# An earlier end of one block's attention and another dealing of the last logits, in a fused attention, gated product and expert kernel

## The chip, the cores and the metric

The kernel runs on one core of one Trainium2 chip. Its time is the device time of one execution in microseconds (us), and the median of several executions is compared. Before the change it is 1007.12 us (three runs, 1005.93 to 1008.37). The profile of before is of an execution of its own that took 1008.56 us.

## The reference

Three layers follow each other, on 3072 tokens (4 batches of 768) of width 512 (8 heads of 64):

```python
for t in range(S):                                   # decayed linear attention
    state = gamma * state + einsum('bhd,bhe->bhde', k[:, :, t], v[:, :, t])
    y[:, :, t] = scale * einsum('bhd,bhde->bhe', q[:, :, t], state)
x = y in (token, head*dim) order                     # 3072 x 512
x = ((x @ w_a) * (x @ w_b)) @ w_out                  # d_ff 1536
e_idx = argmax(x @ w_gate)                           # top 1 of 8 experts
gate_w = softmax(x @ w_gate)[e_idx]
eom = sigmoid(x @ w_output_gate)[e_idx]
out[token] = gate_w * eom * (relu(x @ w1[e_idx]) @ w2[e_idx])   # d_ff 1024
```

All in fp32 accuracy. The choice of the expert depends on small differences of logits, so the kernel works at that accuracy all the way to them.

## The kernel before

**Products.** Every fp32 operand of a big product is split into a high part that TensorE takes in one pass and a low part (the rest). `mm3` then makes three matmuls of each (lines 111, 112 and 113: high by high, high by low, low by high). A split is a cast on ACT and a subtraction on DVE: for the x of a block `split` in `x_steps` (ACT L695, DVE L696), for the gated product `gate` (DVE L579 and L587, ACT L584), for an expert's weights L462 and L463.

**Blocks.** The tokens are four blocks: two of 512 tokens and two of 1024. A loop over j handles the first two blocks. For each of the 12 slices f of d_ff it makes the *up products*: `proj` by w_a (12 matmuls), then by w_b (12), the gate, and `down` of the f before (12 matmuls into four accumulators). After each of these three stands a `slot()`: 36 slots in a loop. At a slot, `spread` hands out steps of other work. Each line of steps has a first and a last slot, and at slot s a step is handed out while the share of steps done is less than the share of the way between the two. The steps of a line are closures that issue instructions, so this decides the place of each instruction in every engine's program. Nothing is moved afterwards: each engine works through its own list in order.

**What is handed out in the loop j=1.** The attention of block 2 (`attention_steps(2)`: scores sc, mask m, state, outputs y on PE, copies on ACT, joins `xraw<-xraw,y` and the decayed operands qd and vd on DVE or POOL) and the routing of the first 512 tokens, `route(0, 4, False)`: 32 dot products for the logits on DVE (`dot`, L342), then `s_m` (largest logit, choice, index ix, exp, counters), then a gather from `w_output_gate` by ix for each tile of 128 tokens (`s_g`, an indirect DMA on POOL, tile wx), a dot product with what it brought (`s_o`, L342 again), and the rest (`s_e`; `s_r`, a rank matmul rp at L401; `s_s`, the scatter into a table tab_d).

**Blocks of sums.** The two blocks of 1024 tokens use a product of sums: seven products of quarters in place of eight, with x operands B11, B21, U1, U2, B22, U3 and U4. `x_steps` forms U1 to U4 by subtractions on DVE (L690) and splits all seven. `block_of_sums` makes, for each f, the seven products (6 matmuls each) with the `down` tiles of f-1 between them, and a slot after each: 84 slots. The sums a, b and later on DVE (L748, L770, L776, L787) release the two accumulators p0 and p1 to the next products. Each product of block 2 also needs a `unit`, sums of the weights (POOL makes wsum, ACT L664 and DVE L665 split it). `later_pass` does the other half of the down product. In before, x of block 2 is formed at slots 27 to 31 (B21 and B11), at the end of the last f (five steps) and in the first slots of the block of sums (four steps).

**Last logits.** The logits of the last 512 tokens are made on PE (`route(20, 4, True)`: transposes pt, products lp, ACT copies lg, then `s_m` and so on), one step after each half of the up products of expert 0's first 256 rows (`up2`), whose tokens are known by then. Then two turns (PE transposes pg of a gathered tile xg, L887, the split ACT L889 and DVE L890) of the next rows of expert 0, which need the table's index (idx, DMA from tab_d) and the gather xg from x. `load_expert` splits the expert's weights (L462, L463) and loads the ones after next.

## Time and profile before

| | |
|---|---|
| median of three runs | 1007.12 us |
| profiled execution, its own time | 1008.56 us |
| span of its profile | 1006.5 us |
| mean granted TensorE clock over the span | 0.987 of full speed |
| PE busy | 962.7 us (96%) |
| DVE busy | 602.6 us (60%) |
| ACT busy | 361.9 us (36%) |
| POOL busy | 249.9 us (25%) |
| DMA moved | 217.58 MB |

Read it so: PE is busy for all but some 44 us of the span, and a part of the rest is at the start and the end. So what is to be looked at are the single waits of PE in the middle, each named with the engine that ended it, and the stretches in which the granted clock fell after them. In the rows below, a number in brackets is the idle time of the engine before an instruction, with what ended it; PEclk is the granted clock as a share of full speed (2.4 GHz; 0.5 is the lower level, 1.2 GHz).

### The profile page before, as it was taken

The page shows a single profiled execution, that of the slowest core. Times are in us where ns is not written, and L with a number is a line of the kernel's source. Part 1 is how long each engine was busy: PE and PEld are TensorE (multiplying, and loading weights), DVE is VectorE, ACT ScalarE, POOL GpSimd, SP SyncE. Part 2 cuts the span into 40 slices and gives each one's busy share as a digit, 9 for nine tenths or more (in the row PEclk, how much of TensorE's full clock was granted, in tenths as well). Part 3 has the DMA queues.
Part 4 walks back from the last instruction along what each step waited for, and adds up shares of the span by engine and source line. Part 5 has one row for each costly group of instructions (what it writes and reads, how often), then busy time and mean ns, then how long its engine had stood idle before and what let it go on. Part 6 is the DMA issues. An engine that isn't in the chain of part 4 may idle for free. (4 is left out here: it accounts for less than half of the span.)

```text
span 1006.5 us, 19402 instructions
## 1 busy us (share of the span) xinstructions
PE 962.7 (96%) x7248; PEld 797.6 (79%) x7249; DVE 602.6 (60%) x1213; ACT 361.9 (36%) x668; POOL 249.9 (25%) x238
## 2 busy tenths in 40 slices
PE   6899999998889999999999999999899999999997
PEld 5688888886678777878787787878799988889886
DVE  4899966785655777657386586444365544445531
ACT  2677752222322222334211112333354434344431
POOL 4211002124434554520012212221321120221311
PEclk9899999999999999999999999999899999999999
DMA  6999979786379876828666865471564552545620
GB/s 237 352 326 310 312 261 359 242 271 243 143 257 374 282 236 227 258 107 295 226 234 210 282 237 180 166 212 45 179 213 136 175 177 86 186 143 155 212 73 29
DMA packets 77253, 217.58 MB, mean 216 GB/s; under 512 B 13230, under 2 KB 22702, under 8 KB 75569
## 3 DMA queue, kind: packets, MB, share of 16 engines
q1 hardware_dynamic: 69840, 196.34, 57.7%
q0 software_dynamic: 6704, 18.93, 5.5%
q8 instruction: 82, 1.34, 0.5%
q10 hardware_dynamic: 576, 0.56, 0.2%
q14 instruction: 51, 0.41, 0.1%
HBM read 165.41 MB, written 51.30 MB: 215 GB/s over the span
## 5 line engine op out<-in xcount | busy, mean ns | idle before, releaser
L941 DVE TENSOR_TENSOR ew<-wraw,ew 128x512 fp32r<-128x512 f32 x112 | 77.1, 690 | 56.0 <-ACT ew L940 55.5
L342 DVE SCALAR_TENSOR_TENSOR junkd<-x2r,wcol 128x512 bf16<-128x512 f32 x128 | 99.9, 780 | 2.4
L111 PE MATMUL acc<-xe,ew 128*128 128x384 f32 (+4 forms) x288 | 98.4, 342 | 0.6 <-issue 0.6
L905 DVE SCALAR_TENSOR_TENSOR hs<-acc,hs 128x384 fp32r<-128x384 f32 (+4 forms) x72 | 39.0, 542 | 98.4 <-ACT hs L904 98.4
L113 PE MATMUL acc<-xe,ew 128*128 128x384 f32 (+4 forms) x288 | 95.4, 331 | 0.0
L112 PE MATMUL acc<-xe,ew 128*128 128x384 f32 (+4 forms) x288 | 95.3, 331 | 0.0
L111 PE MATMUL p<-U,unit 128*128 128x512 f32 x192 | 78.1, 407 | 11.8 <-ACT a L742 4.2
L940 ACT CAST ew<-wraw 128x512 fp32r<-128x512 f32 x112 | 68.8, 616 | 56.9 <-PE acc L113 52.8
L927 POOL DMA_INDIRECT out<-y,idx x27 | 27.4, 1016 | 230.2 <-ACT y L926 154.5
L777 POOL TENSOR_TENSOR later<-later,b 128x512 f32<-128x512 f32 x24 | 37.5, 1563 | 173.8 <-DVE b L776 173.8
L111 PE MATMUL p<-xs,ar 128*128 128x512 f32 x192 | 78.2, 408 | 0.1
L113 PE MATMUL p<-xs,ar 128*128 128x512 f32 x192 | 76.1, 396 | 0.0
L112 PE MATMUL p<-xs,ar 128*128 128x512 f32 x192 | 75.9, 395 | 0.0
L111 PE MATMUL acc<-wos,gs 128*128 128x512 f32 x192 | 75.8, 395 | 0.0
L113 PE MATMUL p<-U,unit 128*128 128x512 f32 x192 | 75.5, 393 | 0.0
L112 PE MATMUL p<-U,unit 128*128 128x512 f32 x192 | 75.4, 393 | 0.0
L904 ACT ACTIVATE hs<-acc 128x384 fp32r<-128x384 f32 (+4 forms) x72 | 34.4, 478 | 113.9 <-PE acc L113 113.7
L113 PE MATMUL acc<-wos,gs 128*128 128x512 f32 x192 | 74.9, 390 | 0.0
L112 PE MATMUL acc<-wos,gs 128*128 128x512 f32 x192 | 74.8, 390 | 0.0
L789 ACT CAST gs<-a 128x512 fp32r<-128x512 f32 x24 | 14.9, 621 | 138.2 <-DVE a L787 127.0
L111 PE MATMUL p<-B,unit 128*128 128x512 f32 x144 | 57.5, 399 | 2.0 <-DVE a L787 2.0
L111 PEld LDWEIGHTS acc<-xe,ew 128*128 128x128 f32 x288 | 54.6, 189 | 3.8 <-issue 1.0
(201 smaller groups left out, 2277.8 us busy)
## 6 DMA issues: line engine op xcount, KB each, us to landing
wraw<-in_ex SPq DMA_DIRECT2D x64, 512.0 KB, 4.1
wos<-wos_d SPq DMA_DIRECT2D x39, 512.0 KB, 5.9
wide<-in_w_ab SPq DMA_DIRECT2D x24, 512.0 KB, 5.5
q_d<-unit SPq DMA_DIRECT2D x24, 512.0 KB, 6.4
unit<-q_d SPq DMA_DIRECT2D x12, 1024.0 KB, 5.7
qk<-in_qk SPq DMA_DIRECT2D x23, 512.0 KB, 6.3
vk<-in_vk SPq DMA_DIRECT2D x23, 512.0 KB, 7.0
q_d<-ar SPq DMA_DIRECT2D x36, 256.0 KB, 4.8
```

Of the source, the lines that this page charges most:

```text
L111: pe.matmul(outp, lhsT=wh, rhs=rh, start=start, stop=False, skip_group_check=more)
L112: pe.matmul(outp, lhsT=wh, rhs=rl, start=False, stop=False, skip_group_check=more)
L113: pe.matmul(outp, lhsT=wl, rhs=rh, start=False, stop=stop, skip_group_check=more)
L342: dve.scalar_tensor_tensor(junk, x, 1.0, y, op0=ALU.mult, op1=ALU.mult, accum_out=out)
L777: pool.tensor_tensor(g2, g2, b2, op=ALU.mult)
L789: act.copy(gs[:, 0], a1)
L904: act.activation(h[:, 0, :n], p[:, :n], AF.Relu)
L905: dve.scalar_tensor_tensor(h[:, 1, :n], p[:, :n], 0.0, f32(h[:, 0, :n]), op0=ALU.max, op1=ALU.subtract)
L927: st = pool.indirect_dma_start(out=out[:, :], out_offset=bass.IndirectOffsetOnAxis(ap=ix[:, 1:2], axis=0), in_=y, in_offset=None, bounds_c ...
L940: act.copy(ew[f][:, part, 0], t[:, part])
L941: dve.tensor_tensor(ew[f][:, part, 1], t[:, part], f32(ew[f][:, part, 0]), op=ALU.subtract)
```

## The change

1. In the loop j=1 the attention's last slot is 25 in place of 30. `x_first` (B21, B11) has slots 22 to 25, and `x_rest` (the nine other steps of x) is a line of its own with slots 26 to 34. No step of x is left at the end of the last f or in the block of sums.
2. The second half of `s_m` becomes a step of its own, `s_c`. Where the logits come from DVE, the gathers of wx are followed by more empty steps before the dot products that read them: five between the first pair's dots and the second pair's.
3. In `block_of_sums` the last f makes down tile 2 of f-1 between U3 and U4, and only tile 3 after U4.
4. In block 2 the attention of block 3 and the routing have slots 0 to 78 and 12 to 82.
5. In the last logits one step is handed out after each quarter of the up products for f = 0 and 1, after every second quarter from f = 2. The loads of the weights of slices 5 to 7 are steps among them, and the two turns come after all up and down products, one right behind the other.

```diff
--- before.py
+++ after.py
@@ -352,6 +352,13 @@
             dve.tensor_reduce(top, first, op=ALU.max, axis=AX.X)
             oh = st["oh"] = small("oh", BF16)
             dve.tensor_tensor(oh, first, over_e(top), op=ALU.is_equal)
+            st["mx"] = mx
+            if not by_pe:
+                ix = st["ix"] = small("ix", I32, (4,))
+                dve.tensor_scalar(ix, top, -1.0, 8.0, op0=ALU.mult, op1=ALU.add)
+
+        def s_c():
+            l8, mx, oh = lg[:, :, :8], st.pop("mx"), st["oh"]
             less = small("less")
             dve.tensor_tensor(less, l8, over_e(mx), op=ALU.subtract)
             ex = st["ex"] = small("ex")
@@ -361,9 +368,6 @@
                 dve.tensor_tensor(both, lg[:, :, 8:], oh, op=ALU.mult)
                 st["og"] = small("og", shape=(4,))
                 dve.tensor_reduce(st["og"], both, op=ALU.add, axis=AX.X)
-            else:
-                ix = st["ix"] = small("ix", I32, (4,))
-                dve.tensor_scalar(ix, top, -1.0, 8.0, op0=ALU.mult, op1=ALU.add)
             cs = st["cs"] = small("cs", BF16)
             dve.tensor_copy(cs[:, 0], ohsum)
             for t in range(1, n):
@@ -433,18 +437,18 @@
             out = [bank((s_t, 0))]
             for t in range(1, n):
                 out.append(bank((s_t, t), (s_l, t - 1)))
-            return out + [bank((s_l, n - 1)), s_m, s_e, bank((s_r,)), s_s]
+            return out + [bank((s_l, n - 1)), s_m, s_c, s_e, bank((s_r,)), s_s]
         out = [lambda: (s_w(), s_x()), s_w] + [none] * 6
         for e in range(E):
             for t in range(n):
                 out.append(lambda t=t, e=e: dot(st["x2", t], cols[e // 2][:, e % 2], lg[:, t, e : e + 1]))
             if e % 2:
                 out.append(s_w)
-        out += [lambda: (s_m(), s_g(0), s_g(1)), none, none, none]
+        out += [lambda: (s_m(), s_g(0), s_g(1)), none, s_c] + [none] * 4
         for t in range(n):
             out.append(lambda t=t: (s_o(t), t + 2 < n and s_g(t + 2)))
-            if t % 2:
-                out += [none, none]
+            if t == 1:
+                out += [none] * 5
         return out + [s_e, bank((s_r,), (s_s,))]
 
     rawq = {}
@@ -779,8 +783,8 @@
                 low1()
                 load_weights(f + 2)
             slot()
-            if f and not last:
-                down(j, f - 1, [2, 3])
+            if f:
+                down(j, f - 1, [2] if last else [2, 3])
             if last:
                 gd = later_split(KEPT[0])
             product(q, u, 0, "U4", False)
@@ -790,7 +794,7 @@
             dve.tensor_tensor(gs[:, 1], a1, f32(gs[:, 0]), op=ALU.subtract)
             gt[j, f] = gs
             if last:
-                down(j, f - 1, [2, 3])
+                down(j, f - 1, [3])
             if fresh:
                 store_unit(2 * f + 2)
             else:
@@ -1147,10 +1151,10 @@
 
         for j in range(2):
             n, tiles = 512, [3, 0, 1, 2] if j else [0, 1, 2, 3]
-            lines = [(attention_steps(j + 1), 0, 30)]
+            lines = [(attention_steps(j + 1), 0, 25 if j else 30)]
             if j:
                 x_first, x_rest = x_steps(2)
-                lines += [(route(0, 4, False), 2, 30), (x_first, 27, 31)]
+                lines += [(route(0, 4, False), 2, 31), (x_first, 22, 25), (x_rest, 26, 34)]
             slot, flush = spread(lines)
             for f in range(NF1):
                 last = f == NF1 - 1
@@ -1191,9 +1195,6 @@
                     flush()
                     if j == 0:
                         split_x(1, n)
-                    else:
-                        for s in x_rest[:3]:
-                            s()
                 if f > 0:
                     down(j, f - 1, tiles)
                 if j == 0:
@@ -1205,8 +1206,6 @@
                 if last:
                     if j:
                         make_unit(1)()
-                        for s in x_rest[3:5]:
-                            s()
                         next_wos()
                     down(j, f, tiles)
                 slot()
@@ -1218,7 +1217,7 @@
 
         sync.dma_start(wos_d[NF1 - 1], f32(wos[1, NF1 - 1]))
         store_unit(1)
-        slot, flush = spread([(x_rest[5:], 0, 4), (attention_steps(3), 4, 78), (route(4, 4, False), 14, 82)])
+        slot, flush = spread([(attention_steps(3), 0, 78), (route(4, 4, False), 12, 82)])
         gd = block_of_sums(2, slot)
         flush()
 
@@ -1257,7 +1256,7 @@
         hs = {}
         nothing = lambda: None
         todo = route(20, 4, True)
-        todo = [*todo[:6], nothing, todo[6], nothing, *todo[7:], count]
+        todo.insert(-2, nothing)
 
         def after():
             load_idx0(2)
@@ -1270,23 +1269,24 @@
         def sizes_known():
             n_e.extend(nc.values_load(cnt[0:1, e : e + 1], min_val=0, max_val=T) for e in range(E + 1))
 
-        todo += [after, *[nothing] * 6, sizes_known, lambda: turn((0, 2), xst(0), 0), lambda: turn((0, 3), xst(0), 128)]
-
         def next_todo():
             if todo:
                 todo.pop(0)()
 
+        todo += [count, nothing, lambda: load_expert(5), nothing, nothing, lambda: load_expert(6), nothing, after]
+        todo += [lambda: load_expert(7), *[nothing] * 8, sizes_known, lambda: turn((0, 2), xst(0), 0), lambda: turn((0, 3), xst(0), 128)]
+        load_expert(4)
         for f in range(NF2 + 1):
             if f < NF2:
-                up2(f, xst(0), LEAD, LEAD, ks=range(2))
-                next_todo()
-                up2(f, xst(0), LEAD, LEAD, ks=range(2, KD))
-                hs[f] = relu(f, LEAD)
-                next_todo()
+                for k in range(KD):
+                    up2(f, xst(0), LEAD, LEAD, ks=[k])
+                    if f < 2 or k % 2:
+                        if k == KD - 1:
+                            hs[f] = relu(f, LEAD)
+                        next_todo()
             if f > 0:
                 down2(f - 1, hs.pop(f - 1), [128, 128], 2)
                 next_todo()
-            load_expert(f + 4)
         while todo:
             todo.pop(0)()
         y = ytile()
```

Three places show how the instructions move; between them the order is the same but for such shifts. The first is DVE at the end of the up products, from the join of the attention's output to the splits of x (B is B21 and B11, og<-x2r,wx the dot products with the gathered rows; g_sb and gs are a gate). Before:

```order
L253 TENSOR_TENSOR xraw<-xraw,y 128x2x2x64 x2
L152 TENSOR_TENSOR qd<-qk,dec 128x512
L161 TENSOR_TENSOR vd<-vk,vtab 128x512
L579 TENSOR_TENSOR g_sb<-p_3090,a_sb 128x512
L587 TENSOR_TENSOR gs<-g_sb,gs 128x512
L342 SCALAR_TENSOR_TENSOR junkd,og<-x2r,wx 128x512 x2
L220 TENSOR_TENSOR m<-sc,mask 128x256 x2
L223 TENSOR_TENSOR state<-state,sc 128x128 x4
L342 SCALAR_TENSOR_TENSOR junkd,og<-x2r,wx 128x512 x2
L696 TENSOR_TENSOR B_3204<-xraw,B_3204 128x1024
L579 TENSOR_TENSOR g_sb<-p_3207,a_sb 128x512
```

After:

```order
L358 TENSOR_SCALAR ix<-top 128x4
L700 TENSOR_TENSOR B_3092<-xraw,B_3092 128x1024
L253 TENSOR_TENSOR xraw<-xraw,y 128x2x2x64 x2
L363 TENSOR_TENSOR less<-lg,mx 128x32
L372 COPY cs<-ohsum 128x8
L374 TENSOR_TENSOR cs<-cs,oh 128x8 x3
L375 TENSOR_TENSOR ohsum<-cs,oh 128x8
L700 TENSOR_TENSOR B_3159<-xraw,B_3159 128x1024
L583 TENSOR_TENSOR g_sb<-p_3185,a_sb 128x512
L591 TENSOR_TENSOR gs<-g_sb,gs 128x512
L342 SCALAR_TENSOR_TENSOR junkd,og<-x2r,wx 128x512 x2
L694 TENSOR_TENSOR xraw<-xraw 128x1024 x2
```

The last join L253 stood behind all four dot products (it is the row after this piece and the two of its gate); now it stands ahead of them, both splits and a gate are between the index ix and the first two of them, and U1 and U3 are formed behind these.

The second place is DVE where the up products end and the first f of the block of sums begins (U is the split of U1 to U4, L665 or L669 a unit of weights, L748 or L752 the sum a). Before:

```order
L665 TENSOR_TENSOR unit<-wsum,unit 128x2x256
L579 TENSOR_TENSOR g_sb<-p_3390,a_sb 128x512
L587 TENSOR_TENSOR gs<-g_sb,gs 128x512
L690 TENSOR_TENSOR xraw<-xraw 128x1024 x2
L696 TENSOR_TENSOR U_3412<-xraw,U_3412 128x1024
L665 TENSOR_TENSOR unit<-wsum,unit 128x2x256
L690 TENSOR_TENSOR xraw<-xraw 128x1024
L696 TENSOR_TENSOR U_3430<-xraw,U_3430 128x1024
L607 COPY x_3450<-acc_2155 128x512
L696 TENSOR_TENSOR B_3481<-xraw,B_3481 128x1024
L748 TENSOR_TENSOR a_3473<-a_3473,p_3466 128x512
```

After:

```order
L700 TENSOR_TENSOR U_3369<-xraw,U_3369 128x1024
L694 TENSOR_TENSOR xraw<-xraw 128x1024
L669 TENSOR_TENSOR unit<-wsum,unit 128x2x256
L700 TENSOR_TENSOR U_3406<-xraw,U_3406 128x1024
L583 TENSOR_TENSOR g_sb<-p_3409,a_sb 128x512
L591 TENSOR_TENSOR gs<-g_sb,gs 128x512
L669 TENSOR_TENSOR unit<-wsum,unit 128x2x256
L611 COPY x_3460<-acc_2197 128x512
L220 TENSOR_TENSOR m<-sc,mask 128x256 x2
L223 TENSOR_TENSOR state<-state,sc 128x128 x3
L752 TENSOR_TENSOR a_3483<-a_3483,p_3476 128x512
```

Between the last gate and the first sum a stood six subtractions and splits of 1024 columns, a unit and a copy, and three more of x behind it; now all of x stands before the last gate, and behind this come a unit, a copy, and m and state of block 3's attention.

The third place is ACT in the last logits (ew is a split of weights, hs the relu of an up product, cnt the sizes of the experts, xe the cast of a turned tile, y an output). Before:

```order
L462 CAST ew<-wraw 128x2x512
L904 ACTIVATE hs<-acc_7135 128x256
L462 CAST ew<-wraw 128x2x512
L904 ACTIVATE hs<-acc_7134 128x256
L904 ACTIVATE hs<-acc_7135 128x256
L904 ACTIVATE hs<-acc_7134 128x256
L1271 TENSOR_LOAD cnt x8
L889 CAST xe<-pg 128x4x128
L904 ACTIVATE hs<-acc_7135 128x256
L889 CAST xe<-pg 128x4x128
L926 ACTIVATE y<-p_7218,idx 128x512
```

After:

```order
L466 CAST ew<-wraw 128x2x512
L908 ACTIVATE hs<-acc_7134 128x256
L466 CAST ew<-wraw 128x2x512
L908 ACTIVATE hs<-acc_7135 128x256
L466 CAST ew<-wraw 128x2x512
L908 ACTIVATE hs<-acc_7134 128x256
L908 ACTIVATE hs<-acc_7135 128x256
L1270 TENSOR_LOAD cnt x8
L893 CAST xe<-pg 128x4x128 x2
L930 ACTIVATE y<-p_7255,idx 128x512
```

The two casts xe stood one relu apart, the first of them ahead of the relu of the last up product; now both stand behind the sizes and the last relu, one right behind the other.

## Rows read from the trace of the kernel before

**Rows 1.** Page, part 1: busy us, share of the span, instructions.

```profile
PE 962.7 (96%) x7248; PEld 797.6 (79%) x7249; DVE 602.6 (60%) x1213; ACT 361.9 (36%) x668; POOL 249.9 (25%) x238
```

**Rows 2.** PE timeline, 240 to 285: start, length, idle before, releaser.

```profile
241.11 0.39 PE L112 MATMUL acc<-wos,gs 128*128 128x512 f32 x1
...
241.33 0.39 PE L113 MATMUL acc<-wos,gs 128*128 128x512 f32 x1
...
245.54 0.18 PE L401 MATMUL rp<-oh,tri 128*128 128x32 bf16 x1 [3.81 <-DVE xraw L253]
...
272.86 0.50 PE L111 MATMUL p<-U,unit 128*128 128x512 f32 x1 [3.65 <-ACT a L742]
...
275.67 0.80 PE L111 MATMUL p<-U,unit 128*128 128x512 f32 x1 [0.38 <-DVE a L748]
...
284.63 0.47 PE L111 MATMUL p<-U,unit 128*128 128x512 f32 x1 [2.69 <-issue]
```

**Rows 3.** Windows: us, PE, PEld, DVE, ACT, POOL busy, PEclk, DMA, GB/s.

```profile
246.00:250.00 4.00, 4.00 (x12) 3.14 (x11) 1.90 (x6) 0.01 (x1) 2.52 (x2) 0.57 0.66 199
273.00:277.00 4.00, 3.62 (x9) 2.42 (x10) 3.21 (x4) 2.29 (x3) 0.00 (x0) 0.57 0.87 335
709.00:714.00 5.00, 4.88 (x19) 4.53 (x20) 1.81 (x3) 1.56 (x3) 0.00 (x0) 0.52 0.72 250
```

**Rows 4.** DVE timeline, 238 to 270, columns as in rows 2.

```profile
238.97 1.34 DVE L342 SCALAR_TENSOR_TENSOR junkd<-x2r,wx 128x512 bf16<-128x512 f32 x1 [4.79 <-DMA wx<-in_wog,ix]
...
241.34 0.69 DVE L342 SCALAR_TENSOR_TENSOR junkd<-x2r,wx 128x512 bf16<-128x512 f32 x1 [1.02 <-DMA wx<-in_wog,ix]
...
245.07 0.75 DVE L253 TENSOR_TENSOR xraw<-xraw,y 128x256 f32<-128x256 f32 x2
...
268.03 1.76 DVE L690 TENSOR_TENSOR xraw<-xraw 128x1024 f32<-128x1024 f32 x1
```

**Rows 5.** The tile wx: its gathers' time from issue to landing.

```profile
DMA to landing us min/median/max: 3.3/4.2/7.8
```

**Rows 6.** Line L152 on DVE: ns min/median/max, first and last start.

```profile
L152 DVE TENSOR_TENSOR qd<-qk,dec x10: 681/684/1835, 5.3 to 226.6; 128x512 f32<-128x512 f32 x10
```

**Rows 7.** Windows, one f of the up products, columns as rows 3.

```profile
213.50:224.00 10.50, 10.50 (x106) 8.30 (x104) 9.40 (x29) 1.91 (x4) 2.46 (x2) 1.00 0.72 240
```

**Rows 8.** PE timeline, both blocks of sums, their waits.

```profile
442.41 0.50 PE L111 MATMUL p<-U,unit 128*128 128x512 f32 x1 [0.85 <-DVE b L776]
...
557.30 0.50 PE L111 MATMUL p<-B,unit 128*128 128x512 f32 x1 [0.70 <-DVE a L787]
...
620.81 0.50 PE L111 MATMUL p<-B,unit 128*128 128x512 f32 x1 [1.30 <-DVE a L787]
```

**Rows 9.** PE timeline, expert 0's first rows.

```profile
702.56 0.28 PE L113 MATMUL acc<-xe,ew 128*128 128x256 f32 x1
...
709.12 1.08 PE L887 MATMUL pg<-ident,xg 128*128 128x128 f32 x4 [6.28 <-DMA xg<-x_d,idx]
...
715.69 0.28 PE L111 MATMUL acc<-xe,ew 128*128 128x256 f32 x1
```

**Rows 10.** DVE timeline, last logits and the turns.

```profile
687.59 1.22 DVE L463 TENSOR_TENSOR ew<-wraw,ew 128x1024 fp32r<-128x1024 f32 x1 [3.83 <-ACT ew L462]
...
691.94 1.21 DVE L463 TENSOR_TENSOR ew<-wraw,ew 128x1024 fp32r<-128x1024 f32 x1
...
693.83 0.17 DVE L413 CAST si<-sf 128x4 int32<-128x4 f32 x1
...
710.86 0.69 DVE L890 TENSOR_TENSOR xe<-pg,xe 128x512 fp32r<-128x512 f32 x1 [10.06 <-ACT xe L889]
```

**Rows 11.** ACT timeline, last logits and the turns.

```profile
686.44 0.17 ACT L323 COPY lg<-lp 128x16 f32<-128x16 f32 x1 [2.11 <-PE lp L322]
...
710.24 0.59 ACT L889 CAST xe<-pg 128x512 fp32r<-128x512 f32 x1 [9.90 <-PE pg L887]
```

**Rows 12.** POOL timeline, the gather of the first 128 rows.

```profile
705.60 0.99 POOL L865 DMA_INDIRECT xg<-x_d,idx  x1 [5.63 <-DMA idx<-tab_d]
```

## The prediction, made before the changed kernel ran

> **What bounds the kernel now.** The page's first part comes first: PE is busy for 96% of the span, and DVE, the next, for 60% [rows 1]. So the time is the length of PE's program plus PE's waits. The change adds and removes no matmul, and only waits, and what the clock does after them, can move. The second view is the list of PE's waits, followed in the PE timeline to their places. Four of them lie where the change works: 3.81 us ahead of the rank matmul at the end of the up products; 3.65, 0.38 and 2.69 us in the first f of the block of sums [rows 2]; 0.85, 0.70 and 1.30 us inside the blocks of sums [rows 8]; and 6.28 us ahead of the first turn in the last logits [rows 9]. The third view is the windows behind the long waits: for 4.0 us after the first, 4.0 us around the second and 5.0 us after the last the granted clock was 0.57, 0.57 and 0.52 on average, which is mostly the lower level of 1.2 GHz [rows 3]. PE was working at full clock before each of them and had stood still for 3 to 6 us. So a long wait costs twice: itself, and the lost part of the clock, 4.0 us of work x 0.43 = 1.7, 3.62 x 0.43 = 1.6 and 5.0 x 0.48 = 2.4 us.
>
> **Why these waits are there.** The first: the DVE timeline shows DVE standing 4.79 and 1.02 us for the gathered rows wx, in front of its dot products [rows 4]. Behind them in DVE's program stand a split of x, a gate and the last join of the attention, and PE's rank matmul, which takes the accumulator bank that this join's operand frees, came when it was done (245.07 + the first part of its 0.75). The gathers take 3.3 to 7.8 us from issue to landing [rows 5], and three hand-outs were between their issue and their reader. The second: DVE and ACT are forming x (subtractions and splits of 1.2 us and more each [rows 4, 10]) just when PE needs the sums that free its two accumulators. The last: the table's scatter follows si at 693.83 [rows 10], the index load and the gather of xg follow that, and the gather is issued at 705.60 after 5.63 us of waiting for the index [rows 12]; PE's up products had ended at 702.56 + 0.28 = 702.84 [rows 9].
>
> **The sum, part by part** (of the profiled execution, 1008.56 us, of which the span is 1006.5).
>
> *End of the up products.* The last join stands ahead of the dot products now, so the 3.81 us go with the 1.7 us of clock behind it: 5.5 us. What is late next: at the new density of steps (attention over 25 slots in place of 30) the scores of the next step come at three places only one product, 12 matmuls of 0.22 to 0.23 us [rows 2], 2.8 us, after the outputs of the step before. In those 2.8 us must fit a copy on ACT, a join of 0.75 [rows 4], and qd and vd of 0.68 each [rows 6]; with about 0.6 for the copy (a 512-column cast takes 0.59 [rows 11]) these are 2.7. Each place can cost from 0 (DVE free) to 1.2 us (qd at its longest, 1.835 [rows 6]); I take 0.3 each, near the median, about 1.0 in all. Net 4.5, between 1.9 and 5.5.
>
> *Start of the block of sums.* All nine steps of `x_rest` stand before the last gate. The 3.65 + 0.38 + 2.69 = 6.7 us and the 1.6 us of clock can go: 8.3 us. Late next are two things. U4 of the first f follows U3 with no down tile between (as for every first f), and must wait for the sum b: about as at the last f of a block, 0.85 [rows 8], I take 0.9. And the last gate has the split of U3, a subtraction, a unit and the split of U4 ahead of it on DVE, each about 1.2 us (a 1024-column split takes 1.21 or 1.22 [rows 10]), some 4.9 us against the 2.8 us of the product beside them; the down product of f = 10 (2.8 us more) hides most, 0.7 us may show (0 to 1.5). Net 6.7, between 5.5 and 8.0.
>
> *Blocks of sums.* The last f had 0.85 us of waiting for b [rows 8] in block 2 and the same in block 3; a down tile (3 x 0.23 = 0.7 us) now lies between: 2 x 0.7 = 1.4. The waits of 0.70 and 1.30 us for a [rows 8] come from dot products that stood for wx; with more empty steps in between both go, 2.0. Against it: attention and dots sit in other slots, and a burst of m, state and a dot before b's sum costs as much as such waits do now; 0.9. Net 2.5, between -0.5 (bursts at four places more) and 4.5.
>
> *Last logits.* Ahead of the last logits' product stand 9 fewer up matmuls of 0.12 and no down matmuls in place of 6 of 0.23: 2.4 us, of which I take 2, since each product now follows its transpose's copy closely. So the last lg, at 686.44 [rows 11], comes at 684.5. The split that stood ahead of the largest logit (from 687.59 for 1.22 us) goes too, and another (691.94, 1.21 us) that stood between it and si [rows 10]. The choice can start at 684.7 in place of 688.8, and si comes 4.1 + 1.2 = 5.3 us earlier; I take 4.6, because relu steps stay between. All that follows si hangs on DMAs and moves along: the turn that started at 709.12 [rows 9] could start at 704.5. PE has from 702.84 still 6 up matmuls (0.7) and 12 down matmuls (2.8) ahead of the turns, which now stand last: 706.3. So the wait of 6.28 and the 2.4 us of clock go: 8.7. What comes: the second turn's cast on ACT (0.59 [rows 11]) and its low part on DVE (0.69 [rows 10]) with their handing over, 1.9 us, are followed at once by up products that read them, where before 12 down matmuls lay between; and the logits' four products can each wait some 0.1 us (0 to 0.3) for their copies, 0.4. Net 6.4, between 1.2 (the gather not earlier, below) and 7.5. Checked from the end: the up products behind the turns start at 706.3 + 1.0 for two turns + 1.9 = 709.2 in place of 715.69 [rows 9], 6.5 earlier.
>
> Sum: 4.5 + 6.7 + 2.5 + 6.4 = 20.1. The profiled execution would take 1008.56 - 20.1 = 988.5. The median of before is 1.44 below its profiled execution, so the forecast is **987.0 us**.
>
> **What hides the moved DVE work.** All steps of x are DVE instructions of 1.2 us and now run in slots 22 to 34, beside attention, gates and dots. They cost nothing only while DVE keeps up. In the busiest f of the up products DVE is at work for 9.40 of 10.5 us, and PE for all of it at full clock [rows 7]. A fifth more attention per slot, if attention is as much as half of DVE's work there, makes 0.9 us: 10.3 of 10.5. So there is just room, and the cover is thin. What could break it the trace shows in single rows: the subtraction took 1.76 us at 268.03 [rows 4], against 1.2 for splits of the same size, and qd once 1.835 against a median of 0.684 [rows 6], while POOL was at work. The Trainium skill speaks against the move here: its GPSIMD Engine Reference (Key points) says that GpSimd shares its SBUF interfaces with VectorE and contends with VectorE instructions that have two SBUF inputs, as all of these have. By that rule each of the eleven steps of x could take up to 0.54 us longer beside POOL (1.76 - 1.22), 6 us of DVE's time; the rows agree in single cases. My sum takes 0 of it for PE, since no PE instruction but a gate's down product reads behind these steps, and keeps the rest for the rivals.
>
> **The rivals.** (a) *The gather is not earlier.* The index load and gather wait for something other than si (SP's loads of weights, or the landing of the scatter). Then xg comes at 709.1, PE arrives at 706.3 and waits 2.8 us, pays the 2.4 of clock and the 2.3 of new waits: the term is 8.7 - 7.5 = 1.2 in place of 6.4, and the time 992.2. For it: 8 us lie between si and the landed index already. Against it: that chain's start moves by two splits that can be seen. Chance 0.13. (b) *wx still comes late and holds the splits.* DVE stands 4.8 + 1.0 us [rows 4] at the first dots as before, now in front of U1 to U4; the last gate and the first products come late by what the 1 us of slack per f does not take back, about 5.4: 992.4. Gathers of up to 7.8 us [rows 5] speak for it, the distance against it: a slot is some 3.5 us [rows 7], and seven of 62 steps over 29 slots are 11.5 us, where four of 58 over 28 were 6.8. 0.10. (a) and (b) together: 997.6, 0.05. (c) *Slower: DVE becomes the bound in slots 4 to 34.* It decides from the point where DVE's work per f passes PE's 10.5 us. To eat the 20.1 us in the seven f's from slot 4 to 24 it must pass by 2.9 us per f, 13.4 us of DVE work; five stretched instructions per f (qd's 1.15 or the subtraction's 0.54 more) reach 10.3 + 2.7 to 10.3 + 5.8 = 13.0 to 16.1 only if all are at or over such a stretch. With 3.6 per f it is 987.0 + 25 = 1012. The median 0.684 of qd speaks against it. 0.04. (d) *It does not do what it says:* the waits move on to the next instruction at each of the four places and the clock falls there all the same: 1007, 0.03.
>
> **How the numbers follow.** Forecast 0.65, (a) 0.13, (b) 0.10, both 0.05, (c) 0.04, (d) 0.03. The likeliest case by itself reaches, with the bounds above added as independent, from 982.5 to 991.5. For 8 in 10 the range takes in (a) and (b) and part of both: 981.5 to 996. About 0.2%, 2 us, can be told from no change; all cases but (c) and (d) are further below, with some of (d) and a mixture of small sums at no change: faster 0.92, same 0.04, slower 0.04.
>
> **What would show it.** Right: no wait of PE over 1.5 us between the last three f's of the up products and the second f of the block of sums, and a granted clock of 1.0 throughout there; the join ahead of the dots; si near 689 less what the earlier parts gave; PE going from the last down product into the turns with no idle time, then one wait of nearly 2 us for xe. Wrong: the outputs of the attention waiting for joins at the new density, DVE idle for wx in front of U1, or the turn still waiting for xg. If the up products from slot 4 to 24 are longer than before with PE waiting on qd, vd or a gate, (c) is the case.

## The result and the profile after

The changed kernel took 998.64 us in the middle of three runs (994.58 to 998.73), where before took 1007.75 beside it: a ratio of 0.9895, with an interval from 0.9855 to 0.9935. Three disturbed runs in the whole record (1587.19 us here, 1587.86 and 5390.08 in two of the experiments) are left out of every time and ratio. So the changed kernel is faster by some 1%, and not by the 2% forecast; 987.0 with a range of 981.5 to 996 was said. Its profiled execution took 998.64 us, with a span of 996.5 in place of 1006.5. The page's first part answers to [rows 1]; PE's work is the same, and its share 97%:

```profile
PE 965.0 (97%) x7248; PEld 797.7 (80%) x7249; DVE 609.2 (61%) x1213; ACT 362.8 (36%) x668; POOL 249.6 (25%) x238
```

The first view to make is a table of stages. Each begins with a matmul that both traces have: the first up product, the first B21 of the block of sums, the B21 of its third f, the first product of a later pass, the first up product of expert 0, PE's last matmul. The lengths are differences of their starts in the PE timelines; the last line goes to the end of the last matmul.

| stage, us | before | changed | difference | forecast |
|---|---|---|---|---|
| both loops of up products | 238.97 | 235.21 | -3.8 | -4.5 |
| block 2, first two f | 34.51 | 26.79 | -7.7 | -6.7 |
| block 2, ten other f | 144.44 | 147.59 | +3.2 | |
| later pass of block 2 | 35.48 | 36.77 | +1.3 | |
| block 3 | 152.38 | 150.24 | -2.1 | -2.5, of these three |
| later pass of block 3 | 43.61 | 46.46 | +2.9 | 0 |
| last logits and experts | 323.89 | 320.89 | -3.0 | -6.4 |

The first two lines are what was forecast, 11.5 us for 11.2. The other five were to bring 8.9 us and cost 2.3. Where they went stands in the PE timeline of the changed kernel; these are the larger of its waits from the end of the up products on (in brackets the idle time and what ended it):

```profile
258.08 0.49 PE L111 MATMUL acc<-wos,gs 128*128 128x512 f32 x1 [0.35 <-ACT gs L588]
...
273.67 0.51 PE L111 MATMUL p<-U,unit 128*128 128x512 f32 x1 [0.78 <-DVE b L780]
...
399.96 0.50 PE L111 MATMUL p<-U,unit 128*128 128x512 f32 x1 [2.68 <-DVE a L752]
...
438.74 0.50 PE L113 MATMUL acc<-wos,gs 128*128 128x512 f32 x1 [0.44 <-DVE gs L794]
...
611.63 0.50 PE L111 MATMUL p<-B,unit 128*128 128x512 f32 x1 [1.37 <-DVE a L791]
...
658.92 0.47 PE L111 MATMUL p<-wos,gd 128*128 128x512 f32 x1 [1.89 <-DMA wos<-wos_d]
...
700.87 1.79 PE L891 MATMUL pg<-ident,xg 128*128 128x128 f32 x8 [1.91 <-issue]
...
703.34 0.58 PE L111 MATMUL acc<-xe,ew 128*128 128x256 f32 x1 [0.68 <-ACT xe L893]
```

The waits of 3.81, 3.65, 0.38 and 2.69 us of [rows 2] are gone, and so is the 6.28 of [rows 9]. New are 2.68 us for the sum a at 399.96 and 1.91 + 0.68 us at the turns; the wait at 658.92 was 1.20 us in before:

```profile
667.49 0.47 PE L111 MATMUL p<-wos,gd 128*128 128x512 f32 x1 [1.20 <-DMA wos<-wos_d]
```

The windows show which of them cost twice (us, PE, PEld, DVE, ACT and POOL busy, granted clock, DMA share, GB/s):

```profile
262.00:300.00 38.00, 37.22 (x401) 29.70 (x402) 16.04 (x32) 11.30 (x23) 15.96 (x18) 1.00 0.94 328
399.00:405.00 6.00, 5.04 (x15) 4.00 (x16) 1.20 (x4) 1.62 (x3) 0.09 (x1) 0.72 0.26 81
658.00:664.00 6.00, 5.08 (x17) 4.02 (x18) 1.64 (x2) 0.65 (x2) 2.14 (x3) 0.72 0.75 146
700.00:708.00 8.00, 6.31 (x28) 5.65 (x29) 2.47 (x4) 2.15 (x4) 3.02 (x3) 0.57 0.61 200
```

The start of the block of sums runs at full clock throughout, where [rows 3] had 0.57. But at each of these three waits the clock fell to 1.2 GHz, for 3.4, 3.4 and 6.8 us. So waits of 1.9 to 2.7 us, with their clock, are the missing gain, and the experiments ask for the cause of each.

### The profile page after: what moved, and what is told of

Its sections match the earlier page's. It is cut to its first block, busy times and chain, and to the rows that moved or that the text cites. A ratio compares the mean times of both kernels' runs of the same rounds, so it can differ in the third digit from the quotient of the medians.

```text
span 996.5 us, 19406 instructions
## 1 busy us (share of the span) xinstructions
PE 965.0 (97%) x7248; PEld 797.7 (80%) x7249; DVE 609.2 (61%) x1213; ACT 362.8 (36%) x668; POOL 249.6 (25%) x238
```

## The experiments

Kernels that ran together share their runs of before, in three sets: 1009.54 us for the changed kernel again, s_c later, the load of slice 7 and the dummy work; 1013.54 for the sizes, the old logits, the steps of x and the first run of the joined kernel; 1009.83 for the other four. Times of different runs are therefore compared by their ratio to before; a ratio compares executions that ran side by side, so it is not the quotient of the two medians. Most of these ratios differ by less than their intervals, so what decides an experiment is the length of a stage and the rows in it.

**The changed kernel again.**

> The changed kernel once more, for its spread. Theory: of the 20 us forecast some 10 are missing at three places, each a wait of PE of 1.9 to 2.7 us that also pulls the granted clock down: 2.68 us for the sum a in f = 9 of block 2 (4.2 us with the clock), 1.89 us for a weight load in the later pass of block 3 (1.7 us more than the 1.20 of before, with the clock 2.9), and 1.91 + 0.68 us at the two turns (2.4 us of clock behind them). Set by the order of the instructions, the first and the last come again within 0.5 us; the middle one hangs on a transfer and may come with 1.2 us and no fall of the clock, 994 to 996 us then, else 998 to 999. Rival (chance): the waits lie elsewhere in another execution and the sum is what stays.

Measured: 994.87 us median (993.05 to 1000.53), 0.9871 of before (0.9829 to 0.9914). The waits came again: 1.84 us at f = 9 of block 2, 1.88 + 0.68 at the turns, both with a fall of the clock, and 1.82 us in the later pass, this time without one. The first is 0.8 us shorter than expected. The waits are set by the order; whether a wait of some 2 us pulls the clock down is not, and the spread of the changed kernel's runs, 7 us, is of the size of a few such falls.

**s_c one step later.**

```diff
-        out += [lambda: (s_m(), s_g(0), s_g(1)), none, s_c] + [none] * 4
+        out += [lambda: (s_m(), s_g(0), s_g(1)), none, none, s_c] + [none] * 3
```

> The changed kernel with s_c one step later, so that in f = 9 of block 2 it stands behind the sum a and not ahead of it. Theory: s_c's instructions of 128x8 and 128x32 took 4.2 us in place of 1.1 because POOL was at work beside them (wsum, qd, vd), and a stood behind them: the wait of 2.68 us falls under 0.5 us, the clock stays up, and the kernel is 4.2 us faster than the changed one, 994.5 us. Rival: the join ahead of s_c or the product before is what is late, the wait stays over 1.5 us and the time at 998.7. Second rival: the stretch moves on to b, which then waits 2 us.

Measured: 991.76 us (988.68 to 994.11), 0.9834 of before (0.9806 to 0.9863), beside the changed kernel's 0.9871. The ten f of block 2 took 141.93 us in place of 147.59 and 146.96, 5 us less, and PE had no wait there over 0.3 us. The intervals of the two ratios overlap, so the stage and its rows carry this. Why is seen by laying the DVE timeline of the changed kernel beside POOL's:

```profile
394.97 0.55 DVE L363 TENSOR_TENSOR less<-lg,mx 128x32 f32<-128x32 f32 x1
...
395.44 0.75 DVE L372 COPY cs<-ohsum 128x8 bf16<-128x8 bf16 x1
...
396.23 2.88 DVE L374 TENSOR_TENSOR cs<-cs,oh 128x8 bf16<-128x8 bf16 x3
...
399.14 0.16 DVE L375 TENSOR_TENSOR ohsum<-cs,oh 128x8 bf16<-128x8 bf16 x1
...
399.23 0.68 DVE L752 TENSOR_TENSOR a<-a,p 128x512 f32<-128x512 f32 x1
```

```profile
394.73 2.13 POOL L652 TENSOR_TENSOR wsum<-wsum 128x256 f32<-128x256 f32 x3
...
396.82 1.27 POOL L152 TENSOR_TENSOR qd<-qk,dec 128x512 f32<-128x512 f32 x1
...
398.05 1.04 POOL L161 TENSOR_TENSOR vd<-vk,vtab 128x512 f32<-128x512 f32 x1
```

Three additions of 128x8 elements (L374) took 2.88 us, where the same line took 0.56 in the first routing; the last of them ends when POOL's vd ends (398.05 + 1.04), and the next instruction, at 399.14, takes 0.16 as always. The sum a, for which PE waits, stood behind them. In the kernel with s_c later the same instructions are stretched in the same way, but a stands ahead of them:

```profile
394.30 0.68 DVE L752 TENSOR_TENSOR a<-a,p 128x512 f32<-128x512 f32 x1
...
396.24 2.41 DVE L374 TENSOR_TENSOR cs<-cs,oh 128x8 bf16<-128x8 bf16 x3
...
398.68 0.16 DVE L375 TENSOR_TENSOR ohsum<-cs,oh 128x8 bf16<-128x8 bf16 x1
```

```profile
397.38 1.04 POOL L161 TENSOR_TENSOR vd<-vk,vtab 128x512 f32<-128x512 f32 x1
```

Again 2.41 us: the second addition ends with vd, the third takes 0.16 behind it, and nobody waits. So the first theory holds. The GPSIMD Engine Reference of the Trainium skill (Key points) says that GpSimd and VectorE contend where a VectorE instruction has two SBUF inputs; these rows agree, and they show its form: a small instruction doesn't run slower throughout, it ends with POOL's. The sum a, with one input from PSUM, took 0.68 us as always. The copy L372, with one input, took 0.75 us too, where it took 0.17 in the first routing.

Where POOL's instructions follow one another without a gap, it can be worse. In the first routing, seven of the eight kernels of the second and third set of runs show one addition of 128x8 that took 4.1 us, until the last of three instructions of POOL (qd, vd and a split of w_out) had ended. In the kernel with one load later, below, the three additions took 4.48 us, the third of them 4.08, and ended with that split (230.13 + 1.29):

```profile
226.98 4.48 DVE L374 TENSOR_TENSOR cs<-cs,oh 128x8 bf16<-128x8 bf16 x3
```

```profile
230.13 1.29 POOL L548 TENSOR_TENSOR wos<-wos 128x512 fp32r<-128x512 f32 x1
```

There PE did not wait for DVE.

**The slots of block 3's attention and of the routing as before.**

```diff
-        slot, flush = spread([(attention_steps(3), 0, 78), (route(4, 4, False), 12, 82)])
+        slot, flush = spread([(attention_steps(3), 4, 78), (route(4, 4, False), 14, 82)])
```

> The changed kernel with the slots of block 3's attention and of the routing of block 2's second part as in before (4 to 78 and 14 to 82), all else as changed, s_c a step of its own. Theory: it was the earlier slots that put s_c ahead of the sum a in f = 9 of block 2, into a stretch in which POOL is at work; here a stands ahead of it again, the wait of 2.68 us and the fall of the clock are gone, and block 2 from its third f on takes 4 to 5 us less than in the changed kernel (142 to 143 us): 0.983 of before. Rival: the split of s_m is to blame wherever it stands, and b or the next a waits 1.5 us or more in its place.

Measured: 994.86 us, 0.9839 of before (0.9791 to 0.9887). The wait for a is gone, and s_c was stretched behind a (two additions of 1.2 and 1.0 us), so the theory holds. The ten f took 144.83 us, not 142 to 143, and PE's timeline has the difference in the attention's products y, here two of three stops:

```profile
396.02 0.36 PE L242 MATMUL y<-m,vd 64*64 64x64 f32 x6 [0.42 <-issue]
396.75 0.36 PE L242 MATMUL y<-m,vd 64*64 64x64 f32 x5 [0.37 <-issue]
```

All eight traces of the second and third set of runs have three such stops of PE in block 2, at nearly the same matmuls of its program (numbers 4255 to 4274, and 4468 to 4470 in all but this one), and the six traces before them have none. With them the matmuls y<-m,vd of the ten f took 6.1 to 6.9 us in place of 4.0 to 4.1. Less these 2.0 us the stage is 142.9, as expected. What stops PE there stays open; lengths of this stage are comparable only within the first six traces or within the other eight. So it is the fourth part of the change, two slots of a table, that put the split step in the wrong place; with the slots of before the split cost nothing here. An unsplit step at the new slots was not run.

**The load of slice 7 out of the scatters' way.**

```diff
-        todo.insert(-2, nothing)
+        todo.insert(7, lambda: load_expert(5))
...
-        todo += [count, nothing, lambda: load_expert(5), nothing, nothing, lambda: load_expert(6), nothing, after]
+        todo += [count, nothing, nothing, nothing, nothing, lambda: load_expert(6), nothing, after]
```

> The changed kernel with the split of slice 5's weights (and so the load of slice 7's) before the s_e step of the last logits, in place of behind the count. Theory: the index load waited for the landing of the scatters because the 512 KB of slice 7 were issued in the middle of them: from si to the index load 10.65 us in place of 8.06. Now the load comes 5 us earlier, that distance goes back to about 8 us, si comes 0.5 us later, and the rows are there when PE comes to the turns: the wait of 1.91 us goes, and if the 0.7 for xe doesn't suffice to pull the clock down, 4.3 us in all, 994.4 us; if it does, 1.9, 996.8. Rival: the 1.91 us is the reading of the eight sizes by PE, the distance shrinks but the wait stays: 998.7.

Measured: 995.21 us, 0.9863 of before (0.9832 to 0.9894), no gain. In the changed kernel si, the index of the table's scatters, was done at 682.10 and the index load was issued 10.65 us later:

```profile
682.10 0.16 DVE L417 CAST si<-sf 128x4 int32<-128x4 f32 x1
```

```profile
686.85 0.33 SPq L459 DMA_DIRECT2D wraw<-in_ex  x1
...
692.75 0.38 SPq L859 DMA_DIRECT2D idx<-tab_d  x1
```

With the load earlier this distance was 7.18 us (680.10 to 687.28), and the gather was issued 7.3 us ahead of the turns in place of 5.2:

```profile
690.59 0.99 POOL L869 DMA_INDIRECT xg<-x_d,idx  x1 [5.21 <-PE acc L113]
```

```profile
697.85 1.06 PE L891 MATMUL pg<-ident,xg 128*128 128x128 f32 x8 [1.91 <-issue]
...
699.64 0.58 PE L111 MATMUL acc<-xe,ew 128*128 128x256 f32 x1 [0.73 <-ACT xe L893]
```

The wait ahead of the turns is 1.91 us as before. So the theory is half right: the 512 KB did stand in the way of the index (rival (a) of the prediction in small), but PE didn't wait for the rows. The rival holds. PE's own queue shows the reading itself: eight loads of one size each (the line gives ns min/median/max of one, then the first and the last start). This is before, then the changed kernel:

```profile
L1271 PEldq TENSOR_LOAD <-cnt x8: 305/308/484, 698.5 to 701.5; - x8
```

```profile
L1270 PEldq TENSOR_LOAD <-cnt x8: 296/306/486, 697.3 to 700.4; - x8
```

They take 3.3 us in both, and in both PE's matmuls go on only when the last has ended: at 701.89 in before, at 700.87 in the changed kernel. What differs is how much work issued ahead of them was still running. In before it lasted until 701.31, in the changed kernel until 698.96:

```profile
701.89 0.36 PE L111 MATMUL acc<-xe,ew 128*128 128x256 f32 x1 [0.58 <-issue]
```

So 0.58 and 1.91 us are the part of the same 3.3 us that shows.

**Work for PE ahead of the turns.** Twenty matmuls that nothing reads, behind the reading of the sizes:

```diff
+        def warm():
+            wp = psg.tile([128, 512], F32, tag="gen", name="wp")
+            for _ in range(20):
+                pe.matmul(wp[:, :256], lhsT=tri[:, 0], rhs=tri.rearrange("p a b -> p (a b)"), start=True, stop=True)
...
-        todo += [lambda: load_expert(7), *[nothing] * 8, sizes_known, lambda: turn((0, 2), xst(0), 0), lambda: turn((0, 3), xst(0), 128)]
+        todo += [lambda: load_expert(7), *[nothing] * 8, sizes_known, warm, lambda: turn((0, 2), xst(0), 0), lambda: turn((0, 3), xst(0), 128)]
```

> The changed kernel with 20 matmuls that nothing reads (bf16, 128x256, some 0.11 us each at full clock) behind the reading of the sizes and ahead of the two turns. They add 2.1 us of work in a place where PE waited 1.91 us. Theory: the clock falls because PE stands still there; with PE at work it stays at 1.0, the turns start at most 0.4 us later, and the 2.4 us lost behind them come back: 996.5 to 997 us. Rival: the clock falls all the same (by what went on before, or by the 0.7 us wait for xe), and the kernel is 0 to 1 us slower than the changed one.

Measured: 997.35 us, 0.9880 of before (0.9854 to 0.9905): no faster. The PE timeline and the window:

```profile
702.33 2.34 PE L1275 MATMUL wp<-tri 128*128 128x256 bf16 x20 [1.70 <-issue]
...
706.28 0.38 PE L111 MATMUL acc<-xe,ew 128*128 128x256 f32 x1 [0.73 <-ACT xe L893]
```

```profile
702.00:709.00 7.00, 5.49 (x44) 4.81 (x44) 1.95 (x3) 1.94 (x4) 1.60 (x2) 1.00 0.50 171
```

The wait, 1.70 us, now stands ahead of the dummy work, which needs no gathered row. So it belongs to the reading of the sizes and not to the turns; the dummy work came behind it and added 2.3 us. The clock stayed at 1.00 in spite of 1.70 and 0.73 us of waiting, where it fell in all six traces that have some 1.9 and 0.7 us of waiting with nothing but the two turns between. So the theory on the clock holds in this one trace, and what was won by it was paid for the filling: last logits and experts took 320.43 us, as in the changed kernel (320.39 beside it).

**The sizes read earlier.**

```diff
-        todo += [lambda: load_expert(7), *[nothing] * 8, sizes_known, lambda: turn((0, 2), xst(0), 0), lambda: turn((0, 3), xst(0), 128)]
+        todo += [lambda: load_expert(7), *[nothing] * 3, sizes_known, *[nothing] * 4, lambda: turn((0, 2), xst(0), 0), lambda: turn((0, 3), xst(0), 128)]
```

> The changed kernel with the reading of the eight sizes five steps earlier, between a down product and the up product of f = 7, where before has it. Theory: the 1.91 us ahead of the turns are this reading (the split of slice 5 moved early brought the rows 4 us sooner and left the wait as it was); at the other place it costs some 0.6 us as in before, the turns come at once, and with only 0.7 us of waiting for xe the clock stays up: 1.3 to 3.3 us faster than the changed kernel. Rival: the reading costs 1.9 us wherever it stands, and nothing is gained.

Measured: 998.74 us (992.57 to 1000.92), 0.9848 of before (0.9794 to 0.9902). PE's timeline at the turns:

```profile
692.69 0.35 PE L111 MATMUL acc<-xe,ew 128*128 128x256 f32 x1 [0.64 <-DVE ew L467]
...
698.78 0.66 PE L891 MATMUL pg<-ident,xg 128*128 128x128 f32 x4 [0.85 <-DMA xg<-x_d,idx]
...
700.11 0.39 PE L111 MATMUL acc<-xe,ew 128*128 128x256 f32 x1 [0.68 <-ACT xe L893]
```

At the earlier place no wait for the reading is left to be seen beside the 0.64 us for a split; at the turns 0.85 us are left, now for the rows, and 0.68 for xe, and the clock stayed up. In the same profile a wait of 1.95 us for a relu at 770.72, in the experts, brought a fall of its own, and the last stage took 322.22 us, more than in the changed kernel. Without that wait and some 1.7 us for its clock (an estimate, 3.4 us of fall at half speed) it would be 318.6, some 2 us less than the 320.89 and 320.39 of the changed kernel, within the 1.3 to 3.3 expected. The time alone can't decide, the rows do.

**The last logits as before.** All of the fifth part taken back (the list, the loop and the place of the loads as in before, s_m and s_c in one step).

```diff
-                for k in range(KD):
-                    up2(f, xst(0), LEAD, LEAD, ks=[k])
...
+                up2(f, xst(0), LEAD, LEAD, ks=range(2))
+                next_todo()
+                up2(f, xst(0), LEAD, LEAD, ks=range(2, KD))
...
```

> The changed kernel with the last logits dealt as in before (one step after each half of an up product, loads at the end of each f, turns between the last quarters), all else as changed. Theory, by the two traces stage by stage: from the first up product of expert 0 to the last matmul before took 323.9 us and the changed kernel 320.9, so this part is worth 3 us and not the 6.4 forecast; this kernel takes 3 us more than the changed one, 998 to 1002, with the wait of some 6 us for xg back. Rival: the changed dealing is worth its 6.4 (or nothing), and the rest of the difference lies elsewhere.

Measured: 1001.93 us, 0.9891 of before (0.9853 to 0.9929). The stage took 326.50 us, 1.29 us of it a wait at 775.50, in the experts, that the earlier traces don't have, and the wait for the rows is back:

```profile
699.17 1.09 PE L891 MATMUL pg<-ident,xg 128*128 128x128 f32 x4 [5.55 <-DMA xg<-x_d,idx]
```

So the fifth part is worth some 4 us here (326.5 - 1.3 - 320.9 = 4.3), 3.0 to 3.5 by the traces before; not 6.4. Beside the next kernel, which has the changed dealing and is of the same set of runs (323.88 us, 2.03 of it two waits in the experts), it is 3.4 (326.5 - 1.3 less 323.9 - 2.0).

**The steps of x back at their old places,** with the attention's early end kept.

```diff
-                lines += [(route(0, 4, False), 2, 31), (x_first, 22, 25), (x_rest, 26, 34)]
+                lines += [(route(0, 4, False), 2, 31), (x_first, 27, 31)]
...
+                    else:
+                        for s in x_rest[:3]:
+                            s()
...
+                        for s in x_rest[3:5]:
+                            s()
...
-        slot, flush = spread([(attention_steps(3), 0, 78), (route(4, 4, False), 12, 82)])
+        slot, flush = spread([(x_rest[5:], 0, 4), (attention_steps(3), 0, 78), (route(4, 4, False), 12, 82)])
```

> The changed kernel with the steps of x where they were in before (the split of B21 and B11 at slots 27 to 31, five of the others at the end of the last f, four in the first slots of the block of sums); the attention still ends at slot 25. Theory: the prediction's second term is right and separate from its first. The end of the up products stays as fast as in the changed kernel, the waits of 3.65 and 2.69 us in the first f of the block of sums come back with their fall of the clock, and from the last f of the up products to the third f of the block it takes 6 to 8 us more: 1001 to 1005 us. Rival: with the attention out of the way DVE has time enough for x there too, the waits come back at less than half, 2 to 3 us, and 997 to 998.

Measured: 1007.27 us, 0.9933 of before (0.9905 to 0.9961), 0.4 to 0.6% over the changed kernel's two ratios; of 1007.75 us it would be 1001.0. The up products took 234.46 us, as short as in the changed kernel, and the first two f of block 2 34.20, as long as in before (34.51). The waits are back, and the fall of the clock, further on than in before: it did not come at the wait of 2.93 us but behind the next one.

```profile
266.66 0.50 PE L111 MATMUL p<-U,unit 128*128 128x512 f32 x1 [0.97 <-ACT a L746]
...
271.25 0.49 PE L111 MATMUL p<-U,unit 128*128 128x512 f32 x1 [2.93 <-DVE a L752]
...
279.02 0.47 PE L111 MATMUL p<-U,unit 128*128 128x512 f32 x1 [2.06 <-issue]
```

```profile
278.00:284.00 6.00, 4.98 (x15) 3.99 (x16) 2.90 (x5) 0.98 (x2) 1.84 (x2) 0.72 0.65 206
```

So the first two terms of the sum are two things, as they were argued: the steps of x give the 7.7 us at the start of the block of sums (7.4 here), and the 4 us of the up products come without them. That these 4 us are the attention's early end is argued from the order, in which the join now stands ahead of the dot products; the longer distance from the gathers to the dots (the second part of the change) could have ended the wait by itself, and the two were not run apart.

**What was learnt, joined.** s_c later, the split of slice 5 early, the sizes ahead of the up product of f = 7, and both turns between the last two down products.

```diff
...
+        todo += [lambda: load_expert(7), *[nothing] * 3, sizes_known, nothing, nothing, lambda: (turn((0, 2), xst(0), 0), turn((0, 3), xst(0), 128))]
```

> The changed kernel with s_c one step later, the split of slice 5 early, the sizes read ahead of the up product of f = 7 and both turns between the last two down products, so that 6 matmuls (1.4 us) cover the split of the second turn. Theory: 4.5 us from s_c, 1.9 - 0.6 = 1.3 from the sizes, 0.7 from xe and 1.7 from the clock that now stays up: some 8 us under the changed kernel of the same runs, 987 to 990. Rival: the turns wait for rows (the second gather lands some 5 us after its issue) or the clock falls as before, 991 to 992, what s_c alone gives.

Measured: 994.71 us, 0.9828 of before (0.9787 to 0.9869), 0.6% under the 0.9891 and 0.2% under the 0.9848 of the same runs, and not the 987 to 990 expected; of 1007.75 us it would be 990.4. Between the up products and the experts the only waits over 1 us were 1.51 for a load of w_out; at the last logits stood one, of the reading, 0.58 us as in before:

```profile
690.33 0.35 PE L111 MATMUL acc<-xe,ew 128*128 128x256 f32 x1 [0.58 <-issue]
```

In the experts two waits of 1.26 and 1.50 us came up that no order here had touched; the other kernels of this set have waits of 0.57 to 1.95 us there, the six earlier traces none over 0.3. And s_c brought less than the 4.5 us counted on: in this set the wait for a was only 1.23 to 1.54 us without it, with no fall of the clock. (It fits that PE's stops in y come some 6 us ahead of a; that they are the reason is not shown.) The ten f took 146.19 us here and 147.44 to 147.97 in the other three kernels of the set, 1.3 to 1.8 us more. So the theory fell short by some 3 us at s_c, and the 2.8 us of waits in the experts came on top. In the next set of runs, where the two waits in the experts shrank to one of 0.40, the stage took 316.72 us, 4 less than in the changed kernel.

> The joined kernel once more, as the measure for the two kernels that change one more thing in it. Both theories: 0.979 to 0.985 of before; the wait for a weight load in the later pass of block 3 again between 1.0 and 2.2 us, with or without a fall of the clock.

Measured: 992.61 us, 0.9809 of before (0.9758 to 0.9860). The load's wait was 2.04 us, with a fall of the clock (0.72 over 658 to 664):

```profile
658.94 0.68 PE L111 MATMUL p<-wos,gd 128*128 128x512 f32 x1 [2.04 <-DMA wos<-wos_d]
```

**One load later.**

```diff
-        slot, flush = spread([(loads, 1, 12), ([fill_gap], 0, 1), (route(16, 4, True), 0, 9), ([first], 5, 6), (turns, 9, 11)])
+        slot, flush = spread([(loads[:2], 1, 6.5), (loads[2:], 7.5, 12.5), ([fill_gap], 0, 1), (route(16, 4, True), 0, 9), ([first], 5, 6), (turns, 9, 11)])
```

> The joined kernel with the third load of expert 0's weights (512 KB) one slot later in the later pass of block 3, behind one more load of w_out. Theory: PE's wait of 1.0 to 2.2 us for wos there comes because this load and the gathers of xg stand in the transfers ahead of it; the wait falls under 0.7 us and can't pull the clock down, 1 to 3 us less than the joined kernel. Rival: the load of w_out is late by its own issue (its buffer comes free late), the wait stays; or it moves to the next slot.

Measured: 989.65 us (986.52 to 991.08), 0.9794 of before (0.9745 to 0.9843), the lowest of all. The later pass of block 3 took 42.93 us in place of 46.61, PE had no wait over 0.3 us in it, and the clock stayed up from the up products to the end of the experts, here in two of the windows:

```profile
621.00:665.00 44.00, 43.76 (x233) 36.48 (x232) 21.00 (x45) 19.10 (x34) 8.62 (x8) 1.00 0.63 213
685.00:710.00 25.00, 24.32 (x158) 21.48 (x158) 12.47 (x24) 11.55 (x24) 8.60 (x8) 1.00 0.63 194
```

The theory holds, by this one trace: what stood ahead of the load of w_out was the load of an expert's weights. The two intervals overlap, so the stage and its rows carry this, not the ratio.

**Without the third part.**

```diff
-            if f:
-                down(j, f - 1, [2] if last else [2, 3])
+            if f and not last:
+                down(j, f - 1, [2, 3])
...
-                down(j, f - 1, [3])
+                down(j, f - 1, [2, 3])
```

> The joined kernel without the third part of the change: in the last f of each block both down tiles 2 and 3 stand behind U4 again. Theory: the tile between U3 and U4 took away the 0.85 us wait for b, but gave back 0.44 us in block 2, where the down product of the last f now comes 0.7 us sooner than its gate is ready; so the part is worth some 0.4 us in block 2 and 0.85 in block 3, and this kernel is 1.2 us slower in the two stages together, which only the profile can tell. Rival, as forecast: 1.4 us.

Measured: 994.07 us beside the joined kernel's 992.61, 0.9832 (0.9766 to 0.9899). The waits for b are back:

```profile
434.38 0.50 PE L111 MATMUL p<-U,unit 128*128 128x512 f32 x1 [0.85 <-DVE b L780]
...
620.15 0.50 PE L111 MATMUL p<-U,unit 128*128 128x512 f32 x1 [0.85 <-DVE b L780]
```

and the joined kernel's wait of 0.47 us for the last gate (0.44 at 438.74 in the changed kernel) is gone. Ten f and later pass of block 2 took 182.28 us where the joined kernel took 181.55, and block 3 150.29 for 150.17, where a wait of 0.90 in the one stands against 0.82 in the other. 0.7 and 0.1 us: less than either expected, and no more can be told from single profiles.

## Why the prediction was wrong

*The end of the up products: right.* Forecast 4.5 us, measured 3.8 (2.9 to 4.1 in the four traces of the next runs). The wait of 3.81 us and its clock went (whether by the join's new place or by the longer distance of the dots stays open); wx was there when its dot products came, so rival (b) did not occur. What was charged, 1.0 us at three places where scores follow outputs after one product, was not there: no wait over 0.3 us between the first f of this loop and its last. In its place came 0.35 and 0.42 us at the last down product, for the gate and for a split of w_out on POOL.

*The start of the block of sums: right,* 7.7 us for 6.7. U4's wait for b was 0.78, for 0.9 said.

*What hides the moved DVE work: right that PE would not wait for it, wrong in the price.* DVE did all of x with the clock at 1.00 and no wait of PE over 0.3 us in slots 4 to 34, and rival (c) did not occur. But a step of x was to take up to 0.54 us longer beside POOL. One of the eleven took 2.3 us in place of 1.22, and one took 4.81, through three instructions of POOL and 1.1 us beyond:

```profile
227.64 4.81 DVE L700 TENSOR_TENSOR B<-xraw,B 128x1024 fp32r<-128x1024 f32 x1 [0.36 <-ACT B L699]
```

Together it was 4.7 us of the 6 allowed for. That the slack took in so long a single step was luck; the same mechanism cost PE time at a place that was not looked at.

*The blocks of sums: this is the first step that failed.* 2.5 us of gain were forecast, with "a burst of m, state and a dot before b's sum costs as much as such waits do now; 0.9". The two blocks and the later pass of block 2 lost 2.3 us (0.2 in the second trace of the changed kernel). The burst that came was s_c's, ahead of a and beside POOL: 2.68 us and a fall of the clock, 4 to 5 us together. The kernel with s_c later gave them back: there the three stages took 4.7 us less than in before, more than the 2.5 forecast. So without this burst the term would have been met, and the failed step is the price of bursts, 0.9. The stretch of DVE beside POOL had been priced, for x alone (1.76 for 1.22), on the largest instructions. On the smallest it was a factor of five here, because they last as long as POOL's, and of 25 where three of POOL's followed one another. The rest: the wait of 1.30 us [rows 8] stayed in some runs (1.37 at 611.63), and 0.44 of the 0.85 came back at the last gate.

*The last logits: the second step that failed.* 6.4 us were forecast, 3.0 to 3.5 came. si came 4.8 us sooner, measured from the first up product (12.3 us for 17.1), as forecast (4.6), and the wait for the rows went. What follows si did not simply move along: the index load was issued 10.65 us behind it where before had 8.06 (the prediction's 8 us were this distance, not the one to the landed index). This hid under the reading of the sizes. Wrong was "the wait of 6.28 and the 2.4 us of clock go". The reading of the sizes, which the list of steps moved from ahead of an up product to directly ahead of the turns, was costed at nothing; of its 3.3 us 0.58 showed at its old place and 1.9 at the new one, where fewer matmuls were left to run beside it. With 0.68 us for xe (1.9 was said) PE stood still for 2.6 us, and the clock fell there once more. The waits came to nearly the forecast sum, 2.6 for 2.3, by chance, since most of it is the reading, which was not in the sum; that they pull the clock down was not reckoned with.

*Beside the sum:* the load of w_out in the later pass of block 3, 1.20 us in before, was 1.89 here with a fall of the clock, 2.9 us. The forecast left that stage out at no cost ("four of them lie where the change works", and this wait was not among the four), and this is the third step that failed. In the thirteen traces after the change the wait was 0.97 to 2.22 us in all but the kernel with the load moved; the clock fell at 1.89, 2.04, 2.06, 2.15 and 2.22, and not at 1.79, 1.82, 1.88 and 2.19. Why it fell in the one and not in the other stays open. So does why the wait grew from 1.20; that it comes from the load ahead is shown by the one kernel that moved this load.

Added up for the profiled execution: 11.5 - 2.3 (blocks) - 2.9 (load) + 3.0 + 0.6 of start-up = 10 us of span. The sum of forecast, 20, is what the kernel with the load moved reached (989.65 us for 1009.83), where the waits that remained were taken away; the agreement is in part chance, since it also takes away the 1.2 us for the load that the forecast had left alone. One bound of the prediction does not come out of its terms: their best cases, added as independent, give 984.2 us at the lower end of the likeliest case and not 982.5, which changes nothing here.

## What to carry to other kernels

When a table of slots or a list of steps moves, look at each engine for what now stands directly ahead of the instruction that PE waits for, the smallest instructions and register reads too: a short instruction beside POOL can last five times its row and more, and a read shows as far as the matmuls issued ahead of it don't last. Price a new wait of some 2 us with and without a fall of the clock: here such waits had one in some executions and not in others. Where single runs differ by more than the question, compare stages between the same matmuls of two traces, and look first whether traces of the same kernel, or of one set of runs, agree on the stage.

## What the runs showed of the hardware

DVE additions of 128x8 elements with both inputs in SBUF took 0.96 us each beside POOL's elementwise work in place of 0.19, and ended with POOL's instruction; one took 4.1 us, until three of POOL's instructions in a row had ended, and a split of 1024 columns took 4.81 us for 1.22. The sum a, with one input in PSUM, took 0.68 us beside POOL. Waits of PE of 1.8 to 2.2 us for the same load were followed by a fall of the granted clock in some executions and not in others; behind one of 2.69 us in before it did not fall, and with the steps of x back one of 2.93 us brought no fall before PE waited again. The reading of eight sizes takes 3.3 us on PE's queue; it showed as 1.7 to 1.9 us of idle time behind the last matmuls of a stage and as 0.6 us between two products. Eight traces of two sets of runs had stops of PE of 0.4 us at nearly the same matmuls, and six earlier traces did not.
